# Two 64-row lists per group in the last mixture of experts, a shorter pair table, and row lists read one at a time

## The chip, the cores and the metric

One core of one Trainium2 chip. The metric is the device time of one execution in microseconds (us); lower is better. PE is TensorE, PEld its weight loads, DVE is VectorE, ACT ScalarE, POOL GpSimd and SP SyncE, which issues most DMAs here.

## The reference

Three layers in a row: windowed attention, a dense layer with softplus (MoE 1), and MoE 2, in which each of 2304 tokens goes to two of 8 experts. The change touches MoE 2 alone:

```python
N, D, E, F = (2304, 512, 8, 1024)
logits = x @ w_gate
noise_scale = np.log1p(np.exp(x @ w_noise))
noisy_logits = logits + noise_scale * noise
top2 = np.argpartition(-noisy_logits, 2, axis=1)[:, :2]
...
for e in range(E):
    for k in range(2):
        mask = top2[:, k] == e
        h = np.maximum(x[mask] @ w1[e], 0.0)
        out[mask] += top2_w[mask, k, None] * (h @ w2[e])
```

With the inputs that the reference draws by default, the experts get 149, 575, 209, 20, 294, 1609, 1034 and 718 rows (4608 in all).

## The kernel before

**Stages.** Attention and MoE 1 are interleaved first. MoE 1's last three chunks of 256 tokens are routed while MoE 2 already runs. Routing writes, for each token, a record (token number, weight) into one of four DRAM lists `rect`, in the row of its expert, with indirect DMAs on POOL (L783).

**Groups.** MoE 2 works on groups. A *pair group* is 256 rows of one expert: x is gathered (L1060), transposed, split into a high and a low float32r part, and multiplied with w1 and w2, themselves split (ACT L1153, DVE L1151), in three products each (`up`, `down`). A *single* is 128 rows of one expert, computed in plain f32 without splits. There are 4 early pairs (from the first 1536 tokens), 14 later pairs, and 7 singles. The first 5 singles are always run: after pairs 1, 4 and 7, and the last two at the very end. Two more stand under a condition that is read from the table; with these inputs exactly 5 are in use. An expert's w1 and w2 come as 8 loads of 512 KB (L1124), into a ring of 24 slots shared with the split copies, and four extra slots.

**Tables.** `late_table` computes on DVE, in one-partition steps (all L882), which expert and which list row each pair starts at (`pairs`), then the same for the singles. The SP queue can read the register of a group only when its table is there, so no load of a late pair is issued before.

**Row lists.** At the first load of a group, `g_rows` reads the row's start into a register (L1040) and issues four small DMAs (L1044), one from each `rect`, in a row, ahead of the group's weights. `merge` on DVE (L1048, L1049) takes the minimum and the sum of the four.

**Order.** The program writes the order of each engine's instructions itself, by a modelled clock (`chain`, `spend`, `need`). On the chip each engine keeps that order: a DVE instruction whose input is late holds all DVE work behind it. In step x of the loop PE does `s1` (w1 product) of item x, `s2` (transposes of a single) of item x-1 and `s3` (w2 product) of item x-2. At the end of a group both halves of 128 rows are scaled (ACT L1267, DVE L1270) and added to `out` by an indirect DMA on POOL (L1261); these additions follow one another.

Of the kernel before, what the change touches and what calls it, by code (L numbers as in the profile page):

```python
# [18 lines left out]
P = 128  # L19
# [91 lines left out]
def moe_chain_kernel(ctx, tc, qk, v, w_in, w_out, w_gate, w_noise, noise, w1, w2, out):  # L111
# [20 lines left out]
    NSING = E - 1  # L132
    NEARLY = 4
    NOPT = 2
# [409 lines left out]
    def down(ys, gh, gl, w, first, last):  # L544
        for tt, y in enumerate(ys):
# [305 lines left out]
    def open_p2():  # L851
        nonlocal p2
        for m in range(NM):
            emitted(("c", m))
        astack.close()
        p2 = ctx.enter_context(tc.tile_pool(name="p2", bufs=2))
        for name, n, base, step in (("jm", NJ, 0, P), ("jpair", NJ // 2, P, 2 * P), ("jfull", NJ // 2, 2 * P, 2 * P),
                                    ("e8", E, 0, 1), ("qe", NEARLY, 0, 1), ("qp", NLATE, 0, 1), ("qs", NSING, 0, 1)):
            t = TB[name] = row(name, [n])
            POOL.iota(t, pattern=[[step, n]], base=base, channel_multiplier=0, allow_small_or_imprecise_dtypes=True)  # L860
# [7 lines left out]
    class Table:  # L868


        def __init__(self, name):
            self.name = name
            self.steps = []
            self.ge = None
            self.big = self.row("big", [E * NJ])
# [61 lines left out]
    def counted(c, name):  # L937
# [4 lines left out]
        tb = Table(name)  # L942
# [5 lines left out]
    def early_table(c):  # L948
        tb, cnt = counted(c, "E")
# [4 lines left out]
        a, b = tb.row("a", [E]), tb.row("b", [E])  # L954
        tb.tensor_sub(b, inc, per)
        tb.tensor_scalar(a, inc, float(NEARLY), None, op0=OP.min)
        tb.tensor_scalar(b, b, float(NEARLY), None, op0=OP.min)
        tb.tensor_sub(a, a, b)
        off = TB["off"] = tb.row("off", [E])
        tb.tensor_scalar(off, a, 2.0 * P, None, op0=OP.mult)  # L960
        chain(*tb.steps, (None, 0.0, None, ("tab", 0), (("scat", c),)), (None, 0.0, pump))

    def late_table(c):
        tb, cnt = counted(c, "L")
        off, e8, qp, qs_ = TB["off"], TB["e8"], TB["qp"], TB["qs"]
        tb.tensor_sub(cnt, cnt, off)
        me = tb.above("me", cnt, TB["jm"], NJ, OP.is_gt)
        per = tb.above("per", cnt, TB["jpair"], NJ // 2, OP.is_gt)
        se = tb.row("se", [E])
        tb.scalar_tensor_tensor(se, per, -2.0, me, op0=OP.mult, op1=OP.add)  # L970
        pinc = tb.upto("pinc", per)
        sinc = tb.upto("sinc", se)
        ptot, stot = pinc[:, E - 1:E], sinc[:, E - 1:E]


        ex, r = tb.first_of(qp, "A", NLATE, pinc, per, off)
        lastr = tb.row("lastr", [E])
        tb.scalar_tensor_tensor(lastr, per, 2.0 * P, off, op0=OP.mult, op1=OP.add)
        all8 = tb.row("all8", [1])
        tb.tensor_scalar(all8, stot, float(E), None, op0=OP.is_equal)  # L980
        ok = tb.row("ok", [NLATE])
        eq = tb.row("eq", [NLATE])
        tb.tensor_tensor(eq, qp, ptot.to_broadcast([1, NLATE]), OP.is_equal)
        tb.tensor_tensor(eq, eq, all8.to_broadcast([1, NLATE]), OP.mult)
        tb.tensor_tensor(ok, qp, ptot.to_broadcast([1, NLATE]), OP.is_lt)
        tb.tensor_add(ok, ok, eq)
        tb.finish("pairs", ex, r, ok, NLATE)
        tb.steps += [(None, 0.0, None, ("tab", 1), (("scat", c),)), (None, 0.0, pump)]


        gq = tb.row("gq", [NSING])
        tb.tensor_sub(gq, qs_, stot.to_broadcast([1, NSING]))
        half = tb.row("half", [NSING])
        tb.tensor_scalar(half, gq, 0.0, None, op0=OP.mult)
        for j in range(1, NSING, 2):
            tb.scalar_tensor_tensor(half, gq, float(j), half, op0=OP.is_equal, op1=OP.add)
        gp = tb.row("gp", [NSING])
        tb.tensor_sub(gp, gq, half)
        tb.tensor_scalar(gp, gp, 0.5, float(NLATE), op0=OP.mult, op1=OP.add)
        exb, rb_ = tb.first_of(gp, "B", NSING, pinc, per, off)  # L1000
        tb.scalar_tensor_tensor(rb_, half, float(P), rb_, op0=OP.mult, op1=OP.add)
        okb = tb.row("okb", [NSING])
        tb.tensor_tensor(okb, gp, ptot.to_broadcast([1, NSING]), OP.is_lt)
        cm = tb.row("cm", [NSING, E7])
        tb.tensor_tensor(cm, jb(sinc[:, :E7], NSING, E7), ib(qs_, NSING, E7), OP.is_le)
        exs = tb.total("exs", cm, NSING)
        rs = tb.of_expert("rs", exs, lastr, NSING)
        own = tb.row("own", [NSING])
        tb.tensor_tensor(own, qs_, stot.to_broadcast([1, NSING]), OP.is_lt)
# [5 lines left out]
        used_ = TB["used"] = tb.row("used", [NSING], I32)  # L1015
        tb.tensor_copy(used_, okb)
        tb.finish("singles", exb, rb_, okb, NSING)
# [4 lines left out]
    ip = is_ = 0  # L1022
    nsure = NSING - NOPT
    while ip < NLATE or is_ < nsure:
        if ip == NLATE or (is_ + 2 < nsure and is_ * NLATE <= (ip - 2) * nsure):
            groups.append((1, "singles", is_))
            is_ += 1
        else:
            groups.append((2, "pairs", ip))
            ip += 1  # L1030
    sure = [len(groups)]
    groups += [(1, "singles", i) for i in range(nsure, NSING)]
    NG = len(groups)
    GR = {}

    def g_rows(g):
# [3 lines left out]
        r0 = SP.value_load(eo[0:1, 1, i:i + 1], min_val=0, max_val=E * T)  # L1040
        rc = tl(p2, [P, 2, 2], I32, "rc", 6, ("gdone", g))
        rk = tl(p2, [P, NCOPY, 2, 2], I32, "rk", 6, ("rows", g))
        for k in range(NCOPY):
            SP.dma_start(rk[:, k, :n, :], rect[k][bass.ds(r0, n * P), :].rearrange("(a p) z -> p a z", p=P))  # L1044

        def merge():

            DVE.tensor_reduce(rc[:, :n, 0], rk[:, :, :n, 0].rearrange("p k a -> p a k"), axis=AX.X, op=OP.min)  # L1048
            DVE.tensor_reduce(f32(rc[:, :n, 1]), f32(rk[:, :, :n, 1]).rearrange("p k a -> p a k"), axis=AX.X, op=OP.add)  # L1049
# [33 lines left out]
    for g, (n, eo, i) in enumerate(groups):  # L1083
        if n == 2:
            for f in range(NW1):
                WJ += [(g, 0, f), (g, 1, f)]
        else:
            WJ += [(g, kind, f) for kind in range(2) for f in range(NW1)]
# [10 lines left out]

    def w2_load():  # L1100
# [3 lines left out]
        g, kind, f = WJ[j]  # L1104
        if g >= sure[0] or ("tab", 2 if groups[g][0] == 1 else int(g >= NEARLY)) not in o_.fin:
# [6 lines left out]
        if g not in REG:  # L1112
            REG[g] = SP.value_load(TB[eo][0:1, 0, i:i + 1], min_val=0, max_val=E - 1)
            g_rows(g)
            if g < 3 or g - 3 in turned:
                g_start(g)
# [7 lines left out]
        SP.dma_start(t, (w2 if kind else w1)[bass.ds(REG[g], 1), f].rearrange("e p n -> p (e n)"))  # L1124
# [60 lines left out]
    H2, Y2 = {}, {}  # L1185

    def s1(g, f):
        n = groups[g][0]
        if n == 2:
            j = WJ.index((g, 0, f // 2))  # L1190
# [6 lines left out]
            gh = tl(mid, [P, CT], F32R, "gh", 4, ("dn", g, f))  # L1197
            gl = tl(mid, [P, CT], F32R, "gl", 4, ("dn", g, f))
# [4 lines left out]
        else:  # L1203
            need(("gx", g, 0))
            ph = tl(psum, [P, 512], F32, "h", 2, ("hr2", g, f))
            for x in range(2):
                j = WJ.index((g, 0, 2 * f + x))
                need(("w2", j))
# [3 lines left out]
                w2_free(j)  # L1212
# [19 lines left out]
    def s3(g, f):  # L1232
# [4 lines left out]
        if n == 2:  # L1237
            j = WJ.index((g, 1, f // 2))
# [3 lines left out]
            down(Y2[g], gh, gl, parts(j, f % 2), f == 0, f == NF1 - 1)  # L1242
            if f % 2:
                w2_free(j)
        else:
            need(("hT", g, f))
            th = H2.pop((g, f))
            for x in range(4):
                ff = 4 * f + x
                j = WJ.index((g, 1, ff // 2))  # L1250
                need(("w2", j))
                mm(Y2[g][0], th[:, x, :], RAW2[j][:, x % 2 * 512:x % 2 * 512 + 512], ff == 0, ff == NF1 - 1)
                if x % 2:
                    w2_free(j)
        mark(("dn", g, f))
        if f == (NF1 if n == 2 else 2) - 1:
            rc = GR[g]["rc"]
            for a in range(n):
                ys = tl(p2, [P, DM], F32, "ys", 4, ("yo", g, a))
                def put(ys=ys, a=a):  # L1260
                    POOL.indirect_dma_start(  # L1261
                        out=out[:, :], out_offset=bass.IndirectOffsetOnAxis(ap=rc[:, a, 0:1], axis=0),
                        in_=ys, in_offset=None, compute_op=OP.add)
# [5 lines left out]
                else:  # L1269
                    ev = ("V", cv(512), lambda ys=ys: DVE.tensor_scalar(  # L1270
                        ys, Y2[g][1], f32(rc[:, 1, 1:2]), None, op0=OP.mult), ("ye", g, 1))
                chain(ev, ("P", 1.1, put, ("yo", g, a)))
# [49 lines left out]
    def phase2(x):  # L1322
        if x < len(items):
# [3 lines left out]
            if g + 1 < sure[0] and f in ((last - 4, last - 2) if last > 1 else (0, 1)):  # L1327
                a = 0 if f in (last - 4, 0) else 1
                if a == 0:
                    need(("gl", g + 1))  # L1330
                if a < groups[g + 1][0]:
                    g_transpose(g + 1, a)
                if a == groups[g + 1][0] - 1:
                    turned.add(g + 1)
                    if g + 4 in REG:
# [4 lines left out]
    for t in range(NT + max(L2, len(items) + 2)):  # L1340
# [28 lines left out]
        if t < NT:  # L1369
# [7 lines left out]
            if NT - 3 < t:  # L1377
                if t == NT - 2:
                    need(("gl", 0))
                g_transpose(0, t - NT + 2)  # L1380
                if t == NT - 1:
                    turned.add(0)
                    if 3 in REG:
# [80 lines left out]
```

## Time and profile before

| | |
|---|---|
| median of 3 runs | 1126.1 us (1125.81 to 1127.66) |
| profiled execution | 1123.13 us, of it 1121.3 us span |
| PE | 1068.9 us busy, 95% of the span |
| PEld | 911.8 us, 81% |
| DVE | 705.5 us, 63% |
| ACT | 615.0 us, 55% |
| POOL | 577.5 us, 52% |
| granted TensorE clock, mean | 0.984 of full |

The span runs from the first to the last instruction of the profiled execution; 1.8 us of its time lie outside. MoE 1's last work and the first groups of MoE 2 meet at about 600 us. An engine's share is a mean over all stages, so the stage has to be looked at. PE's records overlap, so the time that one takes of PE is read from start to start.

### The profile page before, as it was taken

How to read it: one execution, taken by the hardware profiler on the slowest of the kernel's cores; microseconds unless marked ns; L12 is line 12 of the kernel's file. 1: busy time of each engine (PE TensorE's matmuls, PEld its weight loads, DVE VectorE, ACT ScalarE, POOL GpSimd, SP SyncE). 2: the span in 40 equal slices, each digit the busy share in tenths (PEclk: the TensorE clock that was granted, in tenths of full speed). 3: DMA queues.
4: the chain of work that ended last, by engine and by line, in shares of the span. 5: the costliest groups of instructions: out<-in, count | busy, mean ns of one | idle time of the engine just before them, and what ended most of it. 6: DMA issues, size and time to landing. Idle time of an engine off the chain costs nothing.

```text
span 1121.3 us, 21346 instructions
## 1 busy us (share of the span) xinstructions
PE 1068.9 (95%) x7021; PEld 911.8 (81%) x7021; DVE 705.5 (63%) x1914; ACT 615.0 (55%) x1459; POOL 577.5 (52%) x933
## 2 busy tenths in 40 slices
PE   5799999999999999999989997999999999999997
PEld 3577778778888888888878896997997997999984
DVE  7975889888755666666676675653553553565520
ACT  7976878878654444444453553553553553555521
POOL 4767789999876776667765222222222222222112
PEclk8899999999999999999999998999999999999999
DMA  7431454556673222122449638888888888888723
GB/s 291 146 108 67 137 191 170 203 189 220 234 247 123 78 75 74 59 76 76 131 116 350 194 60 309 231 234 269 222 233 267 226 227 261 242 228 230 210 54 38
DMA packets 96560, 198.93 MB, mean 177 GB/s; under 512 B 34048, under 2 KB 44800, under 8 KB 96448
## 3 DMA queue, kind: packets, MB, share of 16 engines
q1 hardware_dynamic: 86112, 176.01, 47.7%
q0 software_dynamic: 10336, 21.54, 9.8%
q8 instruction: 56, 0.92, 0.4%
q14 instruction: 56, 0.46, 0.1%
HBM read 157.82 MB, written 39.69 MB: 176 GB/s over the span
## 4 chain that ended last, share of the span: by engine, by line
PE 67%; DVE 3%; POOL 3%; DMA 3%; issue 2%; ACT 2%; SPq 1%; DVEq 0%; POOLq 0%; ACTq 0%
PE h L188 32%; PE y L188 21%; PE z L188 9%; PE t L199 3%; PE t L188 2%; DMA rawp<-in_moe_w 1%; POOL sl L552 1%; POOL su L552 1%; DVE wlo L1151 1%; DMA rk<-rect 1%; PE t L337 1%; DMA xg<-x1buf,rc 1%; DVE su L585 0%; ACT s L354 0%; POOL cva L499 0%
## 5 line engine op out<-in xcount | busy, mean ns | idle before, releaser
L188 PE MATMUL h<-xh,w 128*128 128x256 f32 x1152 | 238.4, 290 | 4.3 <-DVE sl L580 4.2
L1261 POOL DMA_INDIRECT out<-ys,rc x41 | 80.9, 1973 | 280.2 <-DVE ys L1270 131.8
L1151 DVE TENSOR_TENSOR wlo<-rawp,whi 128x1024 fp32r<-128x1024 f32 x107 | 130.7, 1222 | 133.5 <-ACT whi L1153 111.1
L188 PEld LDWEIGHTS h<-xh,w 128*128 128x128 f32 x1152 | 190.3, 192 | 18.2 <-DVE sl L580 8.9
L1153 ACT ACTIVATE whi<-rawp 128x1024 fp32r<-128x1024 f32 x107 | 113.4, 1060 | 148.5 <-PE h L188 112.5
L188 PE MATMUL y<-w,gh 128*128 128x512 f32 x552 | 178.8, 405 | 0.0
L552 POOL TENSOR_TENSOR su<-sa,su 128x128 f32<-128x128 f32 x288 | 135.3, 491 | 84.2 <-DVE su L585 70.9
L188 PE MATMUL h<-xh,whi 128*128 128x256 f32 x576 | 165.6, 288 | 6.3 <-DVE gl L1200 6.3
L188 PE MATMUL h<-xl,w 128*128 128x256 f32 x576 | 163.9, 285 | 1.9 <-DVE xl L433 1.9
L188 PE MATMUL h<-xl,whi 128*128 128x256 f32 x576 | 163.5, 284 | 0.0
L188 PE MATMUL h<-xh,wlo 128*128 128x256 f32 x576 | 163.4, 284 | 0.0
L552 POOL TENSOR_TENSOR sl<-sl,su 128x128 f32<-128x128 f32 x288 | 136.2, 494 | 4.2 <-DVE sl L580 3.0
L577 ACT ACTIVATE sa<-h 128x256 f32<-128x256 f32 x144 | 54.6, 380 | 142.9 <-PE h L188 93.8
L188 PEld LDWEIGHTS h<-xh,whi 128*128 128x128 f32 x576 | 110.3, 192 | 13.9 <-DVE gl L1200 6.7
L188 PEld LDWEIGHTS h<-xl,whi 128*128 128x128 f32 x576 | 110.4, 192 | 7.1 <-issue 1.4
L188 PEld LDWEIGHTS h<-xl,w 128*128 128x128 f32 x576 | 110.8, 192 | 5.3 <-DVE xl L433 2.4
L188 PEld LDWEIGHTS h<-xh,wlo 128*128 128x128 f32 x576 | 110.4, 192 | 0.0
L188 PE MATMUL y<-w,gl 128*128 128x512 f32 x276 | 108.3, 392 | 0.0
L369 POOL TENSOR_TENSOR s<-s,st 128x256 f32<-128x256 f32 (+2 forms) x144 | 92.6, 665 | 30.0 <-DVE st L360 15.6
L188 PEld LDWEIGHTS y<-w,gh 128*128 128x128 f32 x552 | 94.6, 190 | 16.3 <-issue 2.4
L1060 POOL DMA_INDIRECT xg<-x1buf,rc x41 | 42.4, 1035 | 102.0 <-DVE rc L1049 51.6
L585 DVE TENSOR_SCALAR su<-sa 128x256 f32<-128x256 f32 x144 | 64.6, 449 | 34.7 <-ACT sa L578 33.0
(255 smaller groups left out, 2255.8 us busy)
## 6 DMA issues: line engine op xcount, KB each, us to landing
rawp<-in_moe_w SPq DMA_DIRECT2D x140, 512.0 KB
raw<-in_moe_w SPq DMA_DIRECT2D x44, 512.0 KB
qkT<-in_qk SPq DMA_DIRECT2D x20, 512.0 KB
raw<-in_moe_w_in SPq DMA_DIRECT2D x16, 512.0 KB
raw<-in_moe_w_out SPq DMA_DIRECT2D x16, 512.0 KB
out<-zero SPq DMA_DIRECT2D x19, 256.0 KB
xspill<-xh SPq DMA_DIRECT2D x9, 512.0 KB
xspill<-xl SPq DMA_DIRECT2D x9, 512.0 KB
```

The source lines that it names most:

```text
L188: PE.matmul(o, l, r, start=start, stop=stop)
L199: PE.transpose(o, i, idn)
L337: PE.matmul(ps[j][:nq, x, :n].rearrange("p (s t) -> p s t", t=P), qkT[hd, u % NQK, 0, hp, :nq], qkT[hd, sl, 1, hp, :], start=True, stop=True)
L369: POOL.tensor_tensor(s[:nq, j, :n], s[:nq, j, :n], st[:nq, 3, 2 * x + j:2 * x + j + 1].to_broadcast([nq, n]), OP.mult)
L552: POOL.tensor_tensor(o[:, z], x[:, z], y[:, z], op)
L577: chain(("A", ca(CT), lambda: ACT.activation(a, ph, AF.Abs)), ("A", ca(CT), lambda: ACT.activation(a, a, AF.Exp, scale=-1.0), ("e", t)), ( ...
L585: chain(("V", cv2(CT), lambda: DVE.tensor_scalar(u, a, 1.0, 1.0, op0=OP.add, op1=OP.subtract), None, (("e", t),)), ("P", cg(CT), lambda: b ...
L1060: POOL.indirect_dma_start(out=x, out_offset=None, in_=x1buf[:T - 3 * CT if g < NEARLY else TPAD, :], in_offset=bass.IndirectOffsetOnAxis(a ...
L1151: DVE.tensor_sub(lo, t, f32(hi))
L1153: chain(("A", ca(1024), lambda: ACT.activation(hi, t, AF.Copy), None, (("r2", j),)), ("V", cv(1024), low, ("w2", j)))
L1261: POOL.indirect_dma_start(out=out[:, :], out_offset=bass.IndirectOffsetOnAxis(ap=rc[:, a, 0:1], axis=0), in_=ys, in_offset=None, compute_o ...
```

## The change

- **Halves.** The singles of 128 rows become *halves*: lists of 64 rows. One group (here: a *duo*) holds two of them, of any two experts, on partitions 0 to 63 and 64 to 127. It loads both experts' weights (16 loads). Each product becomes two, with 64 stationary columns each, written to the two halves of the same PSUM tile one after the other. Three duos are always run (after pairs 4, 8 and 12), four stand under conditions. The last group is now pair 13. With these inputs six halves are in use. `out` gets two additions of 64 rows per duo.
- **Pair table.** `pairs` comes out of 12 steps after the copy of the counts, because sums that depend on the early table alone are made earlier. The rest (halves) follows behind it.
- **Row lists.** They are requested two groups further ahead, and `read_rows` issues one list DMA after each weight load, not four in a row. The second half of a duo is read twice (for gather and for addition).
- **Last pair.** Its w2 product is made for the first 128 rows in the usual order; that of the second 128 rows stands in one block behind it. Its `gh`/`gl` live in four ring slots until then, and its w2 splits are kept.

```diff
-    NSING = E - 1
+    NHALF = 2 * (E - 1)
+    NDUO = NHALF // 2
     NEARLY = 4
-    NOPT = 2
+    NSURE = 3
...
     def late_table(c):
-        tb, cnt = counted(c, "L")
...
+        tb, cnt = counted(c, "L", 2 * NJ)
+        tb.ge = TB["ge"]
         per = tb.above("per", cnt, TB["jpair"], NJ // 2, OP.is_gt)
+        pinc = tb.upto("pinc", per)
+        cm = tb.row("Acm", [NLATE, E7])
+        tb.tensor_tensor(cm, jb(pinc[:, :E7], NLATE, E7), TB["marks"], OP.is_le)
+        step = TB["step"]
+        tb.scalar_tensor_tensor(step, per[:, :E7], 2.0 * P, step, op0=OP.mult, op1=OP.add)
+        ex = tb.total("Aex", cm, NLATE)
+        tb.tensor_tensor(cm, cm, jb(step, NLATE, E7), OP.mult)
+        r = tb.total("Ar", cm, NLATE)
+        tb.tensor_sub(r, TB["first"], r)
+        eo = TB["pairs"] = tb.row("eo", [2, NLATE], I32)
+        tb.tensor_scalar(eo[:, 1], r, float(E * T), None, op0=OP.min)
+        tb.tensor_copy(eo[:, 0], ex)
+        tb.steps += [(None, 0.0, None, ("tab", 1), (("scat", c),)), (None, 0.0, pump)]
...
+    for ip in range(NLATE):
+        groups.append((2, "pairs", ip))
+        if ip % 4 == 0 and 0 < ip // 4 <= NSURE:
+            groups.append((1, "halves", ip // 4 - 1))
     sure = [len(groups)]
-    groups += [(1, "singles", i) for i in range(nsure, NSING)]
+    groups += [(1, "halves", i) for i in range(NSURE, NDUO)]
...
+    def pieces(g):
+        n, eo, i = groups[g]
+        return [(2 * i + j, slice(j * P // 2, (j + 1) * P // 2)) for j in range(2)] if n == 1 else [(i, slice(0, P))]
...
+        for i, sl in ps:
+            m = sl.stop - sl.start
+            for k in range(NCOPY):
+                reads.append((g, lambda k=k, i=i, sl=sl, m=m: read(k, i, rk[sl, k, :n, :], m)))
+                if sl.start:
+                    reads.append((g, lambda k=k, i=i, m=m: read(k, i, rk[:m, k, 1:2, :], m)))
...
-        chain(("SP", 0.7 * NCOPY, None))
-        chain(("V", 0.4, merge, ("rows", g)), after=6.0 + 0.7 * NCOPY)
-        GR[g] = dict(rc=rc)
+        def last():
+            chain(("V", 0.4, merge, ("rows", g)), after=6.0)
...
+    def read_rows(g=None):
+        while reads and (g is None or reads[0][0] <= g):
+            x, fn = reads.pop(0)
+            fn()
+            if g is None and not (reads and reads[0][1].__name__ == "last"):
+                chain(("SP", 0.7, None))
+                return
+    NAHEAD = 2
...
-            g_rows(g)
...
+            while rowed[0] < min(g + 1 + NAHEAD, sure[0]) and known(rowed[0]):
+                g_rows(rowed[0])
+                rowed[0] += 1
...
-        SP.dma_start(t, (w2 if kind else w1)[bass.ds(REG[g], 1), f].rearrange("e p n -> p (e n)"))
+        SP.dma_start(t, (w2 if kind else w1)[bass.ds(REG[g][z], 1), f].rearrange("e p n -> p (e n)"))
+        read_rows()
...
                 for kc in range(KC):
-                    mm(ph[:, x * 256:(x + 1) * 256], GR[g]["xT"][:, kc, :],
-                       RAW2[j][:, kc * 256:(kc + 1) * 256], kc == 0, kc == KC - 1)
+                    for j, (i, sl) in zip(js, pieces(g)):
+                        PE.matmul(ph[sl, x * 256:(x + 1) * 256], GR[g]["xT"][:, kc, sl],
+                                  RAW2[j][:, kc * 256:(kc + 1) * 256], start=kc == 0, stop=kc == KC - 1)
...
+            if g == LASTG:
+                down(Y2[g], gh, gl, parts(j, f % 2), f == 0, f == NF1 - 1, [0])
+                later.append((gh, gl, parts(j, f % 2), f == 0, f == NF1 - 1))
...
+                for j, (i, sl) in zip(js, pieces(g)):
+                    PE.matmul(Y2[g][0][sl], th[:, x, sl], RAW2[j][:, x % 2 * 512:x % 2 * 512 + 512],
+                              start=ff == 0, stop=ff == NF1 - 1)
...
+                if g == LASTG and a:
+                    for args in later:
+                        down(Y2[g], *args, [1])
```

## Rows read from the trace of the kernel before

**Rows 1.** By stretch: PE, PEld, DVE, ACT, POOL busy (x), clock, DMA share, GB/s.

```profile
650.00:660.00 10.00, 10.00 (x67) 9.10 (x66) 7.37 (x24) 5.26 (x8) 0.00 (x1) 1.00 0.00 0
...
679.80:686.10 6.30, 0.05 (x1) 0.05 (x1) 2.31 (x9) 0.00 (x0) 1.47 (x1) 0.75 1.06 369
686.10:690.80 4.70, 4.70 (x20) 4.34 (x21) 3.41 (x11) 1.33 (x2) 1.55 (x2) 0.61 1.02 370
690.80:1080.00 389.20, 389.20 (x2415) 344.65 (x2415) 208.26 (x323) 191.86 (x294) 96.20 (x62) 1.00 0.82 230
1080.00:1114.00 34.00, 33.91 (x134) 23.21 (x133) 1.18 (x2) 6.64 (x13) 4.66 (x3) 1.00 0.19 24
```

**Rows 2.** Groups of instructions by line, 680 us to the end: singles' w1 products.

```profile
L188 PE MATMUL h<-rawp,xs 128*128 128x256 f32 x112 | 25.7, 379 | 0.0
...
L188 PE MATMUL h<-raw,xs 128*128 128x256 f32 x48 | 11.2, 379 | 0.0
```

**Rows 3.** Timeline of PE in the first single: start, length, instruction.

```profile
754.84 3.62 PE L188 MATMUL h<-rawp,xs 128*128 128x256 f32 x16
758.30 0.60 PE L199 MATMUL t<-ident,xg 128*128 128x128 f32 x4
...
767.70 3.60 PE L188 MATMUL z<-rawp,th 128*128 128x512 f32 x8
```

**Rows 4.** Timeline of PE, attention: products with 64 stationary columns.

```profile
130.81 0.39 PE L188 MATMUL y<-w,gh 128*128 128x512 f32 x1
131.03 0.40 PE L188 MATMUL y<-w,gl 128*128 128x512 f32 x1
131.36 1.09 PE L188 MATMUL t<-pT,rawv 128*64 128x128 f32 x16
132.38 0.39 PE L188 MATMUL h<-xh,w 128*128 128x256 f32 x1
```

**Rows 5.** Timeline of PEld in the same stretch.

```profile
131.36 0.85 PEld L188 LDWEIGHTS t<-pT,rawv 128*64 128x64 f32 x16 [0.36 <-issue]
```

**Rows 6.** Timeline of DVE: table steps 1, 13 and 34, and one merge.

```profile
639.41 0.14 DVE L882 COPY c_Lcnt<-t 1x8 f32<-1x8 f32 x1
...
645.23 0.24 DVE L882 TENSOR_TENSOR c_LAcm<-c_Lpinc,c_qp 1x98 f32<-1x98 f32 x1
...
661.41 0.16 DVE L882 CAST c_Lpairseo<-c_LAex 1x14 int32<-1x14 f32 x1
...
683.73 0.17 DVE L1048 TENSOR_REDUCE rc<-rk 128x2 int32<-128x8 int32 x1 [9.02 <-DMA rk<-rect]
```

**Rows 7.** Timeline of PE at the end of the last early pair.

```profile
686.05 0.58 PE L188 MATMUL h<-xh,whi 128*128 128x256 f32 x1 [6.28 <-DVE gl L1200]
```

**Rows 8.** Timeline of SP's DMA issues.

```profile
663.54 2.87 SPq L1044 DMA_DIRECT2D rk<-rect  x4
667.00 4.79 SPq L1124 DMA_DIRECT2D rawp<-in_moe_w  x8
673.15 3.23 SPq L1044 DMA_DIRECT2D rk<-rect  x4
```

**Rows 9.** Timeline of POOL: the last indirect DMA into the row lists.

```profile
646.75 1.25 POOL L783 DMA_INDIRECT rect<-rec,pi  x1 [0.30 <-issue]
```

**Rows 10.** The lists' instructions: landing of those indirect DMAs.

```profile
DMA to landing us min/median/max: 2.1/3.4/3.7
```

**Rows 11.** DMA issues from 540 to 755 us: MoE 2's weights, KB each.

```profile
rawp<-in_moe_w SPq DMA_DIRECT2D x49, 512.0 KB
raw<-in_moe_w SPq DMA_DIRECT2D x20, 512.0 KB
```

**Rows 12.** Timeline of POOL's additions to the output.

```profile
1093.01 1.55 POOL L1261 DMA_INDIRECT out<-ys,rc  x1 [17.02 <-DVE ys L1270]
1098.52 1.55 POOL L1261 DMA_INDIRECT out<-ys,rc  x1 [3.96 <-DMA out<-ys,rc]
...
1114.90 1.55 POOL L1261 DMA_INDIRECT out<-ys,rc  x1 [5.75 <-ACT ys L1267]
```

More of the change, by code (lines that the diff above doesn't have):

```diff
@@ L542, in up, with down @@
         return ph
-    def down(ys, gh, gl, w, first, last):
-        for tt, y in enumerate(ys):
+    def down(ys, gh, gl, w, first, last, tts=range(TT)):
+        for tt in tts:
+            y = ys[tt]
             sl = slice(tt * P, (tt + 1) * P)
@@ L953, in early_table @@
         tb.finish("early", ex, r, None, NEARLY)
[L954 to L961, printed above, removed]
+        tb.steps += [(None, 0.0, None, ("tab", 0), (("scat", c),)), (None, 0.0, pump)]
@@ new lines, in early_table @@
+        early, upto = TB["early_of"], TB["early_upto"] = tb.row("of", [E]), tb.row("up", [E])
+        tb.tensor_sub(early, inc, per)
+        tb.tensor_scalar(upto, inc, float(NEARLY), None, op0=OP.min)
+        tb.tensor_scalar(early, early, float(NEARLY), None, op0=OP.min)
+        tb.tensor_sub(early, upto, early)
+        TB["ge"] = tb.ge
+        marks = TB["marks"] = tb.row("marks", [NLATE, E7])
+        tb.tensor_tensor(marks, ib(TB["qp"], NLATE, E7), jb(upto[:, :E7], NLATE, E7), OP.add)
@@ L963, in late_table @@
+        step = TB["step"] = tb.row("step", [E7])
+        tb.tensor_scalar(step, early[:, 1:], -2.0 * P, -float(T), op0=OP.mult, op1=OP.add)
+        first = TB["first"] = tb.row("first", [NLATE])
+        tb.tensor_tensor(first, TB["qp"], early[:, :1].to_broadcast([1, NLATE]), OP.add)
+        tb.tensor_scalar(first, first, 2.0 * P, None, op0=OP.mult)
+        chain(*tb.steps)
     def late_table(c):
-        tb, cnt = counted(c, "L")
-        off, e8, qp, qs_ = TB["off"], TB["e8"], TB["qp"], TB["qs"]
@@ L976, in late_table @@
[L976 to L1005, printed above, removed]
@@ new lines, in late_table @@
+        tb.tensor_tensor(cm, cm, jb(step, NLATE, E7), OP.mult)
[5 more added lines that the diff above has]
+        tb.steps += [(None, 0.0, None, ("tab", 1), (("scat", c),)), (None, 0.0, pump)]
+        off = tb.row("off", [E])
+        tb.tensor_scalar(off, early, 2.0 * P, None, op0=OP.mult)
@@ new lines, in late_table @@
+        he = tb.above("he", cnt, TB["jm"], 2 * NJ, OP.is_gt)
+        se = tb.row("se", [E])
+        tb.scalar_tensor_tensor(se, per, -4.0, he, op0=OP.mult, op1=OP.add)
+        tb.tensor_scalar(se, se, 0.0, None, op0=OP.max)
+        tb.tensor_sub(pinc, pinc, TB["early_upto"])
+        lastr = tb.row("lastr", [E])
+        tb.tensor_scalar(lastr, per, 2.0 * P, None, op0=OP.mult)
+        tb.tensor_sub(per, per, early)
+        ptot = pinc[:, E7:]
+        last = tb.row("last", [1])
+        tb.tensor_scalar(last, ptot, float(NLATE), None, op0=OP.is_ge)
@@ new lines, in late_table @@
+        tb.tensor_mul(se[:, E7:], se[:, E7:], last)
+        sinc = tb.upto("sinc", se)
+        stot = sinc[:, E7:]
+        gq = tb.row("gq", [NHALF])
+        tb.tensor_sub(gq, qs_, stot.to_broadcast([1, NHALF]))
+        gp = tb.row("gp", [NHALF])
+        tb.tensor_scalar(gp, gq, 4.0, None, op0=OP.is_ge)
+        for j in range(8, NHALF, 4):
+            tb.scalar_tensor_tensor(gp, gq, float(j), gp, op0=OP.is_ge, op1=OP.add)
+        quart = tb.row("quart", [NHALF])
+        tb.scalar_tensor_tensor(quart, gp, -4.0, gq, op0=OP.mult, op1=OP.add)
@@ new lines, in late_table @@
+        tb.tensor_scalar(gp, gp, float(NLATE), None, op0=OP.add)
+        exb, rb_ = tb.first_of(gp, "B", NHALF, pinc, per, off)
+        tb.scalar_tensor_tensor(rb_, quart, float(P // 2), rb_, op0=OP.mult, op1=OP.add)
+        okb = tb.row("okb", [NHALF])
+        tb.tensor_tensor(okb, gp, ptot.to_broadcast([1, NHALF]), OP.is_lt)
+        cm = tb.row("cm", [NHALF, E7])
+        tb.tensor_tensor(cm, jb(sinc[:, :E7], NHALF, E7), ib(qs_, NHALF, E7), OP.is_le)
+        exs = tb.total("exs", cm, NHALF)
@@ L1010, in late_table @@
+        tb.tensor_tensor(cm, cm, jb(se[:, :E7], NHALF, E7), OP.mult)
+        s0 = tb.total("s0", cm, NHALF)
+        tb.tensor_sub(s0, qs_, s0)
+        rs = tb.of_expert("rs", exs, lastr, NHALF)
+        tb.scalar_tensor_tensor(rs, s0, float(P // 2), rs, op0=OP.mult, op1=OP.add)
+        own = tb.row("own", [NHALF])
+        tb.tensor_tensor(own, qs_, stot.to_broadcast([1, NHALF]), OP.is_lt)
         for x, y in ((exb, exs), (rb_, rs)):
@@ L1185, in moe_chain_kernel @@
     H2, Y2 = {}, {}
+    HL = [None]
+    later = []
+    LASTG = sure[0] - 1
+    assert groups[LASTG][0] == 2
     def s1(g, f):
```

129 lines of the change are left out of this document (72 added, 57 removed).

## Prediction

> **What bounds the kernel.** I read the share of each engine first, then busy time by stretch, because 95% for PE is a mean over three layers. From 690.8 to 1080 us PE is busy in all of 389.2 us at the full clock, while DVE has 208 us and ACT 192 us of work, and the DMA engines are busy for 0.82 of it [rows 1]. So in this stage PE's issue sets the end; the same holds in the last 34 us, where DMA falls to 0.19. What leaves PE there leaves the span, as long as the DMAs can follow. One hole stands ahead of it: from 679.8 to 686.1 us PE does nothing, and for 4.7 us after that it runs at a granted 0.61, between its two levels of 1.2 and 2.4 GHz [rows 1]. The waits say why: PE waits for `gl` from DVE [rows 7], and DVE has sat 9.02 us in front of a merge, for a row list [rows 6].
>
> **Singles.** The trace has 112 + 48 = 160 records of their w1 product [rows 2]. The code makes 16 such products in a single, and the first single shows 32 records (two stretches of 16), so a product is two records and 160/32 = 5 singles ran: the five that always run, none of the conditional ones. From start to start, 16 records take 758.30 - 754.84 = 3.46 us, 0.216 each [rows 3], so w1 costs 32 x 0.216 = 6.9 us. That row's length, 3.62, runs 0.16 us into the next work; with the same taken off the others, eight w2 records are 3.44 us and four transposes 0.44 [rows 3]. Sixteen w2 records make 6.9 us, twelve transposes 1.3. A single is 15.1 us of PE.
>
> **Duos: how many, and at what price.** The reference's counts, cut as the table cuts them (pairs of 256 while more than 128 rows remain, then 64 at a time), leave 0, 1, 0, 1, 1, 2, 1, 0 halves: six, which is three duos, and no conditional one. The numbers of rows are not times; they only say which code runs.
>
> If the two 64-column products of a duo run side by side, a duo costs PE what a single does. Before has no duo, but attention has such products: 16 records of 128 columns onto 64 output partitions, alternating between both halves. By the single's rate a record of half the columns is 0.108 us; in turn 16 would take 1.73 us, side by side 0.86. The next work starts 132.38 - 131.36 = 1.02 us after the first [rows 4]: side by side, with 0.16 us lost at the exit. The stretch starts 0.33 us after a 512-column product, where the product before it had taken 131.03 - 130.81 = 0.22 [rows 4], so 0.11 is lost at the entry. A duo has four such stretches (two `s1`, two `s3`): 4 x 0.27 = 1.1 us, 3.2 us for three. Ends for this: 0 and 3 x 13.8 = 41.4 us (the second products all in turn, 6.9 + 6.9 per duo). I take 3.2, since attention's is the same form of instruction with half the columns.
>
> The Trainium skill, "TensorE: Matmul & The Clock Gate" (Part 3, The mechanism), says that a weight load overlaps products in flight only when the row group differs, and both halves of a duo use all rows. By that rule the sum would be 15.3 us worse, as the rival on exposed loads works out; the trace speaks against it, since 0.85 us of loads [rows 5] and 0.86 us of products fit into 1.02 us [rows 4].
>
> Sum of the groups: two fewer of 15.1 us, -30.2; drains +3.2.
>
> **Pair table and lists.** Before, 34 steps run from 639.41 to 661.41 us [rows 6], in among other DVE work; step 13 came at 645.23, so the new table's 13 (with the copy) should end 16 us earlier. A second condition then comes last: the lists must be complete. The last indirect DMA into them runs from 646.75 to 648.0 us [rows 9] and lands in 2.1 to 3.7, median 3.4 us [rows 10], so at 651.4. List reads start there and not at 663.54 [rows 8]: 12 us earlier, into DMA engines that before moved 0 GB/s from 650 to 660 [rows 1]. That stretch is free, so the early loads cost nobody.
>
> What is late next? Before, eight weight loads stood in front of the second group's four list reads [rows 8]: the backlog that DVE waited for. Now one load comes between two reads. SP takes 4.79/8 = 0.6 us for a load and 2.87/4 = 0.7 for a read [rows 8], 1.3 for both; a load of 0.524 MB takes 1.42 us at the 370 GB/s of the busy stretch [rows 1]. So SP feeds hardly faster than the DMAs drain, and no backlog grows. But a group's fourth read now stands behind four loads: 651.4 + 1.3 for the register + 4 x 1.3 = 658 us, plus a landing that I bound by 2 us (half of a routing DMA's) and by the 7.3 us of the bad case (676.38 [rows 8] to 683.73 [rows 6]). The merge still gets its place 6 us of model time after the last read. So DVE may stand before the first one for 0 to 7 us. DVE's 9.02 us idle cost PE 6.28 [rows 6, 7]: 2.7 us are covered. Behind a merge stand `gl`, for which PE waits at once, and the split copies.
>
> The old hole cost 6.3 us plus 4.7 x (1 - 0.61) = 1.8 us of clock [rows 1], 8.1 in all. I take back 2 for a new wait of about 4.5 us of DVE: -6. Ends: -8.1, and 0 if a wait of 9 us is merely moved. The remaining table steps (halves) are about as many as were saved, at 0.14 to 0.24 us [rows 6], on a DVE that is idle for 181 of 389 us [rows 1]; the first duo's loads need them, more than two groups ahead of PE. That slack hides them; in one piece, 55 such steps would hold DVE for 8 to 13 us.
>
> **Last pair.** Its 24 late products of 512 columns (0.22 us each at [rows 4], of which I take 0.23 with the edges) keep PE busy for 5.5 us, while the first half is scaled and added. Before, the last addition starts at 1114.90 [rows 12], 0.9 us after PE's end at 1114 [rows 1], and the span ends 6.4 us later. Two additions stand 1098.52 - 1093.01 = 5.5 us apart [rows 12]. So now the first starts 0.9 us after the early half is done, the second could start at 6.4, and its data is ready at 5.5 + 0.9 = 6.4. The end stays; I add 0.3 because the second half is scaled on DVE, not on ACT. If the block did not cover the first addition, it would cost the whole 5.5. Kept splits leave fewer slots ahead: each step still holds the w1 product and half the w2 product. I bound this by 0 and 2 us and take 0, as ACT and DVE are about half idle [rows 1].
>
> **Sum.** -30.2 + 3.2 - 6 + 0.3 = -32.7. The profiled execution took 1123.13 us, of it 1121.3 span; the new one takes 1090.4. The median of the runs lies 3.0 above the profiled execution, so I forecast **1093 us** for the median.
>
> **Rivals.**
>
> *The hole is only moved* (13%). The first list waits for the routing DMA at 651.4 while DVE's merge stands early in its order. For it: its place does not know SP's real pace. Against: an empty DMA queue. Without the -6: 1099 us.
>
> *DMAs bind around duos* (10%). 69 loads are issued by 755 us [rows 11], where the first single begins, and four early and two late pairs have used 48: 21 are ahead. A duo eats 16 in 16 us; at 1.42 us, 16 loads take 22.7. Were they all waited for, each duo costs 7 more: 1093 + 21 = 1114 us. Against: on average 0.82 x 389.2 = 319 us of DMA work [rows 1] plus 8 more loads at 1.42 gives 330 in about 359, a share of 0.92, where stretches show up to 1.06.
>
> *Halves run in turn* (5%), the slower side: each duo's second products add 13.8 us, 1093 + 41.4 = 1134 us. It decides from 11 us per duo on, where the gain of 32.7 is spent. Against it stands attention's stretch [rows 4].
>
> *Weight loads exposed* (4%). A duo has 32 x 2 + 16 x 2 = 96 weight loads; at 0.85/16 = 0.053 us [rows 5] that is 5.1 us, 15.3 for three: 1108 us. Against it: a stretch with half the columns has half the room to hide a load, and yet next to nothing was exposed in it [rows 4]. The rule of the Trainium skill's page on TensorE, named above, is what would bring it about.
>
> *A fourth duo runs* (4%): if a seventh half is in use. It starts cold: 22.7 us of loads, of which PE's 15 overlap in part, and a second tail of 7: about +35, 1128 us, slower.
>
> **Chances and range.** The forecast holds 64%; its own range is 1085 (the whole hole gone and no drains, -2.1 - 3.2, and 2.7 of the covered wait) to 1098. Runs of before spread by 0.2%, so about 2 us either way counts as the same. Faster by over 0.2%: 64 + 13 + 4 and nearly all of the 10, 0.90; same 0.01; slower 5 + 4, 0.09. From 1084 to 1108 leaves out some 5% below, and above it the two slow cases and part of the DMA one, about 14%.
>
> **What would show it.** A w1 stretch of a duo has 32 records of 64 stationary columns: 3.5 us long if they run side by side, 6.9 if in turn. The last `c_Leo` step at about 646 us, list reads from 651. DVE's idle before L1048: under 3 us is right, 9 is the first rival. Around duos no PE wait for `rawp`, DMA share near 0.92. The last two additions 5.5 to 6.5 us apart, the end 7.4 us after PE's last product. I am wrong if PE has holes after 700 us, or if a fourth group of 64-column products appears behind the last pair.

## The result and the profile after

The changed kernel takes 1109.9 us (median of 4 runs, 1108.33 to 1110.49) against 1125.95 for the kernel before on the same chip: a ratio of 0.9858, 95% interval 0.984 to 0.9876. That is 16 us faster where 32.7 were forecast, outside the range of 1084 to 1108. The profiled execution took 1110.49 us, span 1108.5.

The windows of the changed kernel first (per engine busy time and records, then the granted clock, DMA share, GB/s), and two windows of the kernel before:

```profile
540.00:640.00 100.00, 89.24 (x544) 76.82 (x543) 63.54 (x194) 41.50 (x95) 51.97 (x93) 0.91 0.62 193
600.00:620.00 20.00, 16.20 (x82) 14.13 (x82) 12.27 (x43) 5.21 (x12) 10.65 (x17) 0.76 1.01 372
700.00:1090.00 390.00, 389.52 (x2537) 333.42 (x2537) 209.09 (x315) 190.22 (x294) 99.60 (x62) 1.00 0.81 238
```
```profile
540.00:640.00 100.00, 93.41 (x602) 81.36 (x601) 68.47 (x220) 48.54 (x106) 52.42 (x88) 0.98 0.68 219
600.00:620.00 20.00, 19.51 (x130) 16.68 (x129) 11.47 (x33) 8.15 (x16) 7.56 (x8) 1.00 0.91 306
```

The late stage is as forecast: PE full at the full clock for 389.5 of 390 us. But between 540 and 640 us PE has lost 4.2 us of busy time, and the clock went from 0.98 to 0.91; between 600 and 620 it was 0.76, between the levels 1.2 and 2.4 GHz, behind waits for DVE. (The window of 20 us is not quite like for like: before has a slow clock of its own at 590 to 595 us, 0.66, behind a wait shown below. The window of 100 us holds both.) Nothing in my sum lay in that stretch.

To measure stretches I take one product as a marker: the count of rows ahead of each pair table (`t<-mcum,ones`). PE's timeline (start, length, what, idle time ahead of it and its releaser) shows the two markers and the waits between and behind them. Changed kernel:

```profile
539.26 0.18 PE L189 MATMUL t<-mcum,ones 128*128 128x8 bf16 x1 [1.00 <-DVE mcum L771]
561.31 0.39 PE L189 MATMUL h<-xh,w 128*128 128x256 f32 x1 [2.48 <-DVE sl L582]
598.70 0.58 PE L189 MATMUL h<-xh,w 128*128 128x256 f32 x1 [4.18 <-DVE sl L582]
614.46 0.19 PE L189 MATMUL t<-r_mb,tri 128*128 128x8 bf16 x1 [3.63 <-DVE r_mb L718]
654.23 0.18 PE L189 MATMUL t<-mcum,ones 128*128 128x8 bf16 x1 [1.98 <-DVE mcum L771]
678.28 0.39 PE L189 MATMUL h<-xh,whi 128*128 128x256 f32 x1 [0.66 <-DVE gl L1264]
```

In the kernel before, PE's two longest waits between the markers are these:

```profile
589.65 0.38 PE L188 MATMUL h<-xh,w 128*128 128x256 f32 x1 [3.75 <-DVE sl L580]
601.49 0.18 PE L188 MATMUL t<-r_mb,tri 128*128 128x8 bf16 x1 [0.49 <-DVE r_mb L716]
```

So the wait of 4.18 us is not new: it has its counterpart of 3.75 before (and of 3.80 in run 1 below), each time behind a row of weight splits on DVE. New are the 2.48 and the 3.63.

In the kernel before the markers stand at 535.11 and 638.62 us, and its end at 1121.3. So the profiled difference splits in three:

- Up to the early table: +4.15 us. The work there is nearly the same in both. The same marker fell between 537.75 and 540.78 in the profiles of my experiments with the changed kernel, and at 538.03 in that of run 4, which has the order of the kernel before. The profile before was also 3 us faster than the median of its runs. So this is most likely a spread of executions; no run shows it for certain.
- Early table to late table: 103.5 us before, 115.0 after, **+11.5 us**.
- Late table to the end: 482.7 us before, 454.3 after, **-28.4 us**.

Behind the late table most of the prediction holds. The hole of [rows 7] has shrunk from 6.28 to 0.66 us. The table's steps take 655.02 to 661.02, 6.0 us where 5.8 were reckoned; the first list read is issued at 663.01, 8.8 us behind the marker instead of 24.9. The third and fourth are issued only at 670.06 and 671.26, 15.8 and 17.0 behind it, later than the 12.8 of the prediction for complete lists. DVE still waits for them, but 2.57 us in place of 9.02, which is under the 3 that the prediction named as its sign of being right:

```profile
675.42 0.17 DVE L1080 TENSOR_REDUCE rc<-rk 128x2 int32<-128x8 int32 x1 [2.57 <-DMA rk<-rect]
```

One stretch of a duo's w1 products on PE reads so:

```profile
833.32 0.39 PE L189 MATMUL z<-whi,gl 128*128 128x512 f32 x1
833.64 3.67 PE L1276 MATMUL h<-rawp,xs 128*64 128x256 f32 x32
837.24 0.66 PE L200 MATMUL t<-ident,xg 128*128 128x128 f32 x4
```

32 records from start to start take 3.60 us: side by side, against 16 full-width records in 3.46 [rows 3]. A w2 stretch takes 3.58. Duos start at 833.64, 943.77 and 1054.64. A pair takes 23.43 us (from one pair's transposes to the next one's, 997.84 to 1021.27 in the kernel before), so four pairs account for 93.7 us of the 110.1 between the first two duos, and a duo costs 16.4. The prediction had 16.2, the single's 15.1 plus four drains of 0.27; measured, each stretch loses 0.33. The trace has 144 + 48 = 192 records of L1276, three times 64, so three duos ran and no fourth. PE waits for no weights. It waits once for DVE, 0.48 us at 993.03, and the second and third duo stand 0.7 us further apart than the first two.

The time of the early stretch is lost on DVE. Its merges of lists L1080 in the changed kernel:

```profile
560.15 0.17 DVE L1080 TENSOR_REDUCE rc<-rk 128x2 int32<-128x8 int32 x1 [5.43 <-DMA rk<-rect]
598.89 0.15 DVE L1080 TENSOR_REDUCE rc<-rk 128x2 int32<-128x8 int32 x1
605.86 0.17 DVE L1080 TENSOR_REDUCE rc<-rk 128x2 int32<-128x8 int32 x1 [2.03 <-DMA rk<-rect]
614.08 0.17 DVE L1080 TENSOR_REDUCE rc<-rk 128x2 int32<-128x8 int32 x1 [1.75 <-DMA rk<-rect]
```

and those of the same groups before:

```profile
555.19 0.15 DVE L1048 TENSOR_REDUCE rc<-rk 128x2 int32<-128x8 int32 x1
592.51 0.15 DVE L1048 TENSOR_REDUCE rc<-rk 128x2 int32<-128x8 int32 x1
605.46 0.16 DVE L1048 TENSOR_REDUCE rc<-rk 128x2 int32<-128x8 int32 x1
622.63 0.17 DVE L1048 TENSOR_REDUCE rc<-rk 128x2 int32<-128x8 int32 x1 [2.21 <-DMA rk<-rect]
```

9.2 us of DVE waiting now stand where 2.2 stood. Behind the first merge stands `sl`, for which PE then waits 2.48 us, and behind the last two stands `r_mb` (3.63 us). Part of those 3.63 is another thing: between these two merges a DVE step of routing on two columns (`r_g`) took 2.94 us at 608.56, where it took 0.31 before and 0.15 in run 1. What held it is not shown. SP's queue says why the first list is late:

```profile
549.78 0.36 SPq L1177 DMA_DIRECT2D raw<-in_moe_w  x1
551.01 0.40 SPq L1069 DMA_DIRECT2D rk<-rect  x1
...
553.85 0.72 SPq L1177 DMA_DIRECT2D raw<-in_moe_w  x1
554.81 0.38 SPq L1069 DMA_DIRECT2D rk<-rect  x1
```

Each of the four reads goes out behind a 0.524 MB load (two of the four are shown). The last is issued at 554.81, the merge comes free at 560.15. Before, all four were issued ahead of the first load, and the merge did not wait.

The end, in the chain that ended last:

```profile
1091.34 0.70 ACT ys L1346
1092.03 0.27 issue
1092.30 5.97 DMA out<-ys,rc
...
1098.31 1.83 issue
...
1100.35 1.56 POOL out L1339
```

The first half's addition starts 1.0 us after the half is done, where 0.9 was forecast. But the second starts 8.05 us after the first, not 5.5: the first one's DMA takes 5.97 us, and 1.83 us of issue follow. Its data had been ready since 1097.53. From PE's last product, 1096.75, to the end it is 11.75 us, where before it was 7.4.

### The profile page after: what moved, and what is told of

Read it like the earlier page. It is cut to its first block, busy times and chain, and to the rows that moved or that the text cites. A ratio compares the mean times of both kernels' runs of the same rounds, so it can differ in the third digit from the quotient of the medians.

```text
span 1108.5 us, 21426 instructions
## 1 busy us (share of the span) xinstructions
PE 1048.4 (95%) x7045; PEld 886.5 (80%) x7045; DVE 709.8 (64%) x1910; ACT 608.9 (55%) x1447; POOL 581.0 (52%) x932
## 5 line engine op out<-in xcount | busy, mean ns | idle before, releaser
L1205 DVE TENSOR_TENSOR wlo<-rawp,whi 128x1024 fp32r<-128x1024 f32 x111 | 135.6, 1222 | 118.3 <-ACT whi L1207 116.9
L189 PEld LDWEIGHTS h<-xh,w 128*128 128x128 f32 x1152 | 191.3, 193 | 22.3 <-DVE sl L582 12.8
L1207 ACT ACTIVATE whi<-rawp 128x1024 fp32r<-128x1024 f32 x111 | 117.5, 1060 | 135.8 <-PE h L189 114.3
L189 PEld LDWEIGHTS h<-xh,whi 128*128 128x128 f32 x576 | 111.0, 193 | 12.8 <-issue 3.2
L370 POOL TENSOR_TENSOR s<-s,st 128x256 f32<-128x256 f32 (+2 forms) x144 | 93.1, 669 | 30.0 <-DVE st L361 18.9
L189 PEld LDWEIGHTS y<-w,gh 128*128 128x128 f32 x552 | 95.7, 192 | 16.4 <-issue 2.4
L1097 POOL DMA_INDIRECT xg<-x1buf,rc x39 | 44.6, 1144 | 85.6 <-PE h L1276 28.5
L355 ACT ACTIVATE s<-s,st 128x256 f32<-128x256 f32 (+2 forms) x160 | 76.1, 478 | 16.1 <-DVE st L349 15.9
```

The lines of the kernel that those rows point to most:

```text
L189: PE.matmul(o, l, r, start=start, stop=stop)
L355: ACT.activation(s[:nq, j, :n], s[:nq, j, :n], AF.Exp, bias=st[:nq, 0, y], scale=-1.0, accum_out=st[:nq, 1, y])
L370: POOL.tensor_tensor(s[:nq, j, :n], s[:nq, j, :n], st[:nq, 3, 2 * x + j:2 * x + j + 1].to_broadcast([nq, n]), OP.mult)
L1097: POOL.indirect_dma_start(out=x, out_offset=None, in_=x1buf[:T - 3 * CT if g < NEARLY else TPAD, :], in_offset=bass.IndirectOffsetOnAxis(a ...
L1205: DVE.tensor_sub(lo, t, f32(hi))
L1207: chain(("A", ca(1024), lambda: ACT.activation(hi, t, AF.Copy), None, (("r2", j),)), ("V", cv(1024), low, ("w2", j)))
```

## Experiments

All times are medians, each beside the kernel before on the same chip, which took 1127.0 to 1127.7 us in these runs and 1125.95 in that of the changed kernel. Differences from the changed kernel are those of the medians; taken from the ratios they come out up to 2.6 us otherwise.

**1. The merge later.** The theory: merges stand too early in DVE's order for lists that are read between weight loads. The rival: the loads themselves fill the DMA queues. The edit, in `g_rows`:

```
-            chain(("V", 0.4, merge, ("rows", g)), after=6.0)
+            chain(("V", 0.4, merge, ("rows", g)), after=12.0)
```

> The changed kernel (1109.9 us), with each merge placed 12 us of model time behind its last list read, not 6. Merge theory (about 11.5 us were lost ahead of the late table because DVE stands in front of merges whose row lists land late, 5.4, 2.0 and 1.8 us before the first three): those waits vanish, 1099 to 1102 us. Load theory (the loss comes from weights and gathers that start later because list reads stand between the loads, or from added table steps): merges are not the cause, 1108 to 1112 us.

1097.04 us, ratio 0.9724 (0.9694 to 0.9754): 12.9 us faster than the changed kernel (15 by the ratios), by one number, and 2 us past what the theory allowed. Between the tables it is 103.5 us again, as before. Of the early merges one still waits, and PE's busy time in the same 100 us is back:

```profile
560.92 0.17 DVE L1080 TENSOR_REDUCE rc<-rk 128x2 int32<-128x8 int32 x1 [0.73 <-DMA rk<-rect]
```
```profile
540.00:640.00 100.00, 95.93 (x620) 84.13 (x621) 70.54 (x224) 47.64 (x105) 54.14 (x95) 0.97 0.65 212
```

Busy time times granted clock makes 93.1 us of full-speed work in this window, and 81.2 in the changed kernel. By this estimate 11.9 us were lost, of which 6.7 are idle time and the rest is clock.

**2. Lists of a group read in a row**, ahead of the weight loads, with the merge's place written as in the kernel before.

```
-            chain(("V", 0.4, merge, ("rows", g)), after=6.0)
+            chain(("V", 0.4, merge, ("rows", g)), after=6.0 + 0.7 * NCOPY)
...
                 g_rows(rowed[0])
+                read_rows(rowed[0])
+                chain(("SP", 0.7 * NCOPY, None))
                 rowed[0] += 1
```

> The changed kernel with the four list reads of a group in a row again, ahead of the weights of the group at which they are asked for (still two groups ahead), merge 8.8 us behind. Merge theory: lists do not queue behind weights any more, the early waits fall, 1100 to 1104 us. Load theory: the first weights start 5 to 8 us later still, 1112 to 1118 us.

1118.88 us, ratio 0.9937 (0.992 to 0.9954): slower than the changed kernel, and neither theory had the reason. Three groups' lists now make 12 reads in one piece:

```profile
655.19 10.85 SPq L1069 DMA_DIRECT2D rk<-rect  x12
666.28 1.51 SPq L1179 DMA_DIRECT2D rawp<-in_moe_w  x3
```

The early merges still wait 0.72 and 2.48 us, those at 664 to 669 wait 1.46 and 4.61, and PE waits for `gl` behind them and near the duos (4.13 us at 672.57; 0.74, 3.40 and 2.34 at 861.68, 877.06 and 991.70). By the markers the early stretch did gain: 108.6 us between the tables, against 115.0 in the changed kernel and 103.5 before. What was lost lies behind the late table, 466.4 us against 454.3. As both the reads' order and the merge's place differ, this run does not tell the theories apart.

**3. The last pair in order**, without the late block: `s1` and `s3` treat the last group like every other.

```
...
-            if g == LASTG:
-                down(Y2[g], gh, gl, parts(j, f % 2), f == 0, f == NF1 - 1, [0])
-                later.append((gh, gl, parts(j, f % 2), f == 0, f == NF1 - 1))
-            else:
-                down(Y2[g], gh, gl, parts(j, f % 2), f == 0, f == NF1 - 1)
+            down(Y2[g], gh, gl, parts(j, f % 2), f == 0, f == NF1 - 1)
...
```

> The changed kernel without the last pair's late block: both halves' w2 products in the usual order. Tail theory (two additions follow one another about 8 us apart, and the block covers 5.5 us of the first): both halves end with PE's last product, 1114 to 1117 us. Rival (the block covers nothing because the second addition waits anyway): 1108 to 1111 us.

1116.34 us, ratio 0.9893 (0.9857 to 0.9929). So the block is worth 6.4 us by the medians and 4 by the ratios; in the profiles, PE's last product and the end stand 16.3 us apart here and 11.75 with the block, 4.6 less. The prediction said 5.5 would be lost if it covered nothing. The two additions start 7.05 us apart even here, so late data of the second half is not the reason for the distance:

```profile
1100.62 1.56 POOL L1329 DMA_INDIRECT out<-ys,rc  x1 [12.54 <-DVE ys L1339]
1107.67 1.56 POOL L1329 DMA_INDIRECT out<-ys,rc  x1 [5.48 <-issue]
```

**4. The kernel before with a later merge.** If a merge too early is the whole story, before's hole yields to one number too.

```
-        chain(("V", 0.4, merge, ("rows", g)), after=6.0 + 0.7 * NCOPY)
+        chain(("V", 0.4, merge, ("rows", g)), after=18.0 + 0.7 * NCOPY)
```

> The kernel before (1126 us), with each merge 12 us of model time later and nothing else changed. Merge theory: the hole of 6.3 us and its 1.8 us of slow clock were DVE's place in the order alone, 1117 to 1120 us, without any change to tables or reads. Load theory: PE would have waited for the weights of the late pairs anyway, 1124 to 1127 us.

1120.85 us, ratio 0.9946 (0.9929 to 0.9963): 6.7 us from the kernel before without a new table, 0.85 above what was expected. Behind the late marker PE has no wait over 0.4 us for `gl` left, and that part takes 474.5 us in place of 482.7: 8.2 less, what the hole and its clock had cost. Between the tables it takes 2.9 us more than before; PE now waits there once for gathered rows, 1.59 us at 614.87.

**5. Early merges alone, 6. late merges alone.**

```
+            chain(("V", 0.4, merge, ("rows", g)), after=12.0 if g < NEARLY else 6.0)
```

This is the edit of run 5, in the place of run 1's; run 6 has the two numbers the other way round.

> The changed kernel with the merge placed 12 us behind the last read for the four early groups alone; the later ones keep 6. Theory (the early merges cost the 11.5 us between the two tables, later ones next to nothing): 1097 to 1100 us, early table to late table 103 to 105 us of the trace. Rival (late merges cost as well, the slack they lose is given back later): 1102 to 1106.

> The counterpart: merges of the pairs and duos 12 us behind their reads, those of the four early groups at 6. Theory: 1107 to 1110 us, between nothing and 3 us faster than the changed kernel, and early table to late table still about 115 us. Rival (late merges cost as well): 1102 to 1106.

Early alone: 1098.93 us (0.9756, 0.9725 to 0.9787), 103.5 us between the tables. Late alone: 1106.39 (0.9827, 0.9797 to 0.9858), 113.7 us between the tables. The early ones make 11 of the 12.9 us. The late ones' 3.5 are at the rim of what the intervals can tell, just past what I had allowed.

**7. Merges at 18.**

> All merges 18 us behind their last read in place of 12. Theory: DVE waits for no list at 12 any more, so 18 gives nothing: 1095 to 1099 us. Rival (the row gathers now start late, and PE waits for the rows of the next group): 1101 or more, with PE waits for transposed rows or POOL's gathers.

1096.47 us, 0.9737 (0.9707 to 0.9766): the same as at 12. The margin is used up, and gathers do not become late.

**8. The pair table as long as before.** Ahead of its last step, 21 copies that nobody reads, with merges at 12 and at 6:

```
+        spare = tb.row("spare", [NLATE])
+        for _ in range(21):
+            tb.tensor_copy(spare, ex)
         tb.tensor_copy(eo[:, 0], ex)
```

> The changed kernel with merges at 12 us (1097.04 us) and 21 more DVE steps (copies nobody reads) ahead of the end of the pair table, so that it is as long as before, 34 steps. If the shorter table is what closed the hole near the late table, as the prediction has it, the lists come 10 to 16 us later and the hole is back: 1103 to 1106 us, with a PE wait of 4 to 8 us between 660 and 700 us. Rival (the merge's place behind its reads closes it, whenever the table ends): 1095 to 1099, no such wait.

> The same 21 steps in the changed kernel itself, merges at 6 us (1109.9 us). If the shorter table closed the hole: 1116 to 1119 us. Rival (the table's length does not matter): 1108 to 1112.

1103.09 us (0.9795, 0.976 to 0.983) against 1097.04, and 1118.38 (0.9917, 0.9888 to 0.9946) against 1109.9: 6 and 8.5 us (8 and 7 by the ratios). Behind the late marker the profiles differ by 3.2 and 9.0 us. The first list read comes 15 and 16 us later, and the hole is back, 2.76 us long with merges at 12 (4 to 8 had been expected) and, with merges at 6:

```profile
690.07 0.17 DVE L1083 TENSOR_REDUCE rc<-rk 128x2 int32<-128x8 int32 x1 [6.08 <-DMA rk<-rect]
695.82 0.17 DVE L1083 TENSOR_REDUCE rc<-rk 128x2 int32<-128x8 int32 x1 [5.51 <-DMA rk<-rect]
```
```profile
697.99 0.58 PE L189 MATMUL h<-xh,whi 128*128 128x256 f32 x1 [8.31 <-DVE gl L1267]
```

**9. A duo's halves not alternating**, with merges at 12. In w1 four products of one half and then four of the other, in w2 two and two:

```
-                for kc in range(KC):
-                    for j, (i, sl) in zip(js, pieces(g)):
+                for j, (i, sl) in zip(js, pieces(g)):
+                    for kc in range(KC):
...
```

> The changed kernel with merges 12 us behind the reads (1097.04 us by the earlier run), and the products of a duo's two halves no longer alternating: in w1 four products of one half, then four of the other, in w2 two and two. If alternation is what lets the halves run side by side, only products at the boundaries overlap: w1 takes 13 product times of 0.432 us in place of 8 per stretch (+2.2 us), w2 5 of 0.86 in place of 4 (+0.86), so about +6 us per duo and 18 for three: 1112 to 1118 us; with no overlap at all +13.8 per duo, 1138. Rival (the order does not matter, another thing such as the weights sets the 3.6 us): 1095 to 1099, with a w1 stretch still at 3.6 us.

1105.77 us, 0.9816 (0.9786 to 0.9846). Dearer than the rival, and cheaper than either of my numbers: a w1 stretch takes 4.63 us in place of 3.60, a w2 stretch 3.63, as good as alternating. That is 2.2 us per duo, 6.5 of the 8.7 for three; a PE wait of 1.61 us at 1060.74 makes up most of the rest. So products of the two halves still overlap at the boundaries of the blocks. From these rows I worked out how much a boundary gives back, and predicted the next run.

**10. A duo's halves wholly apart**: each stretch all of one half, then all of the other (`for z, (i, sl) in enumerate(pieces(g))` as the outer loop of both stages).

> The changed kernel with merges at 12 us (1097.04 us), each stretch of a duo issued as all 16 w1 records of one half and then all 16 of the other, and in w2 eight and eight. In blocks of 8 records a w1 stretch took 4.63 us in place of 3.60, in blocks of 4 a w2 stretch 3.63 in place of 3.58: a boundary between the halves seems to give back about 0.76 us, 3.5 records of 0.216. If so, one boundary leaves 6.9 - 0.8 = 6.1 us for w1 and 6.9 - 1.5 = 5.4 for w2, +9 us per duo: about 1124 us. If the prediction's price for halves in turn holds (nothing overlaps), 6.9 and 6.9 us, +13.8 per duo: 1138. Rival (PE finds work for the other half however far back it is queued): 3.6 to 4.7 us as before, 1097 to 1107.

1123.78 us, 0.9969 (0.9951 to 0.9987), where 1124 was expected. The stretch:

```profile
821.43 0.39 PE L189 MATMUL z<-whi,gl 128*128 128x512 f32 x1
821.75 6.32 PE L1275 MATMUL h<-rawp,xs 128*64 128x256 f32 x32
828.00 0.66 PE L200 MATMUL t<-ident,xg 128*128 128x128 f32 x4
```

6.25 us for w1 and 5.35 for w2 (6.1 and 5.4 expected): 8.8 us more per duo, 26.5 for three, and the time rose by 26.7 from 1097.04. Nearly the whole gain of the duos hangs on the order of two loops. The second duo, whose halves read differently named tiles in its first stretch, shows what happens at the boundary. The program has 16 records of `raw` and then 16 of `rawp`:

```profile
940.69 3.02 PE L1275 MATMUL h<-raw,xs 128*64 128x256 f32 x13
943.34 0.43 PE L1275 MATMUL h<-rawp,xs 128*64 128x256 f32 x1
943.55 0.38 PE L1275 MATMUL h<-raw,xs 128*64 128x256 f32 x1
943.60 0.38 PE L1275 MATMUL h<-rawp,xs 128*64 128x256 f32 x1
943.76 0.38 PE L1275 MATMUL h<-raw,xs 128*64 128x256 f32 x1
943.82 0.38 PE L1275 MATMUL h<-rawp,xs 128*64 128x256 f32 x1
943.98 0.38 PE L1275 MATMUL h<-raw,xs 128*64 128x256 f32 x1
```

The second half's first record, at 943.34, starts ahead of the last three of the first half (943.55, 943.76 and 943.98). So PE took up products of the other half from behind queued ones of this half, but only about three of them.

## Why the prediction was half right

**Singles and duos: right.** A duo costs 16.4 us where 16.2 were reckoned, and three against five singles make -26.2 where the forecast had -27.0. The rival that halves run in turn is false for this order of products, and its mechanism is real: with the halves apart it cost 26.7 us. The 41.4 of the rival was too much, because one boundary in each stretch still overlaps.

**Weight loads exposed: false, though its time fits.** This rival gave 1108 us, near the 1109.9 measured, so it has to be looked at by its own mark. It asked for 5.1 us of exposed loads per duo; the four stretches of a duo have 14.4 us together, 0.5 more than four stretches of a single at 3.46, and all in all a duo costs 1.3 more than a single. That mark is not met. The rule of the Trainium skill ("TensorE: Matmul & The Clock Gate", Part 3, The mechanism), that a load overlaps only products of another row group, would make these stretches longer; this trace does not agree.

**DMAs bind around duos: false.** PE is busy 389.5 of 390 us, at a DMA share of 0.81; from 830 to 860 us, around the first duo, the share is 0.93 and PE is busy throughout.

**Pair table and the hole: right.** -6 forecast; a PE wait of 0.66 us is left of the hole, and run 8 puts the shorter table at 6 to 8.5 us by the medians, 3.2 and 9.0 by the profiles: with merges at 12 the table matters less. Run 4 adds that the same hole could have been closed by the merge's place.

**The step that failed: "Pair table and lists" priced the new list reads at the late table only.** I reasoned that a group's fourth read now stands behind four loads and that the merge keeps its place 6 us behind the last read, so that DVE "may stand before the first one for 0 to 7 us", and I let 2.7 us of it be covered. That reasoning holds for every group whose list is read, and four groups are read before the late table, in a stretch that I had no row for. There DVE also does MoE 1's and routing's work, and PE waits for DVE at once. Runs 1 and 5 show the price: 12.9 us in all, 11 of them early. It is a wait that takes the place of the one removed, as the first rival has it, but at another place, and the rival's price (6 us) came from the hole alone.

**The tail was mis-sized.** +0.3 forecast, +4.35 measured (11.75 against 7.4). The cover works, as run 3 shows, but I took the distance of two additions from a single row, the last pair's 5.5 us [rows 12]; at the end of the changed kernel it is 8.05. The trace before could have told: of its 14 late pairs that one is the shortest, and in the other 13 the two additions start 7.4 to 10.9 us apart, as here, 7.59 apart with a wait for the first one's DMA:

```profile
1042.39 2.65 POOL L1261 DMA_INDIRECT out<-ys,rc  x1 [8.39 <-DVE ys L1270]
1049.98 1.57 POOL L1261 DMA_INDIRECT out<-ys,rc  x1 [4.94 <-DMA out<-ys,rc]
```

The sum by measured terms: behind the late table -26.2 for the groups, +0.7 between the second and third duo, -7.4 for the hole and its clock (8.1 less what is left) and +4.35 for the tail make -28.5, against -28.4 of span. With the +11.5 ahead of it that is -17.0, against -16.9 beside the spread ahead of the early table. With merges at 12, the kernel takes 1097.04 us, 4 from the 1093 forecast; the tail's 4 us would account for that.

## What to carry to other kernels

When a change re-orders a queue, list every consumer of that queue over the whole kernel, not only the one whose stall is to be cured, and price each where it stands. A place given "so many us behind the request" in an in-order engine has to be set anew when the request's company changes; here one number was worth 13 us. A larger one than needed cost nothing in the changed kernel (run 7), but in the kernel before (run 4) the early stretch became 2.9 us longer. Two independent products that use half the columns each were worth 26.7 us here only when issued in turns of a few.

## What the runs showed of the hardware

- Products on two column halves ran side by side not only when strictly alternating. Blocks of 4 records of 512 columns cost nothing (3.63 us against 3.58), blocks of 8 of 256 columns cost 29% (4.63 against 3.60), and one boundary per stretch left 6.25 of the 6.9 us that serial work would take. A boundary gives back the time of 3 to 3.6 records by these figures; what sets this number was not tried.
- The last of four list reads, each behind a 0.524 MB load, kept its merge until 5.3 us after its issue (554.81 to 560.15), enough to idle DVE for 5.43 us. The damage was not the idle time alone: behind PE's wait the granted clock was 0.74 from 560 to 565 us, and by the estimate above clock makes some 5 of the 12 us that run 1 gave back.
- The two additions of a pair into the same tensor started 7.4 to 10.9 us apart in 13 of the 14 late pairs before and 5.5 in the last; in the changed kernel 8.05 at its end and 6.2 in the pair ahead of that (1067.36 and 1073.58). Those of a duo, of 64 rows each, started 6.3, 6.6 and, in the last duo, 3.8 apart (1079.32 and 1083.13).
